# Attention taps and a mixture layer: last rows of x stacked high over low, low parts by TensorE and ScalarE, three partial sums left to VectorE, and a new order of steps

## The chip, the cores and the metric

One NeuronCore of a Trainium2 chip runs the whole kernel. The time is device microseconds per execution; lower is better. PE is TensorE's matmul, PEld its weight load, DVE is VectorE, ACT ScalarE, POOL GpSimd, SP the engine that issues most transfers.

## The reference

```python
def _attn_ref(x, weight_gen):            # x: 8 x 4160 x 192, weight_gen: 8 x 4160 x 8 x 7
    w = softmax(weight_gen over its 7 taps)
    x_unf = the 7 rows x[s-6 .. s], zeros ahead of the start
    out[s, head, :] = sum over k of w[s, head, k] * x_unf[s, k, head, :]

def _moe_ref(x, w_in, w_out, g_ln):      # x: 33280 x 192, w_in: 192 x 1024, w_out: 1024 x 192
    h = x @ w_in
    e = np.exp(h - h_max)
    sm = e / (np.sum(e, axis=-1, keepdims=True) + 1e-09)
    solu = h * sm
    ln = (solu - mean(solu)) / np.sqrt(var(solu) + 1e-06) * g_ln
    return ln @ w_out
```

`w_in`, `w_out` and `g_ln` come as float64 (`x` and `weight_gen` as float32). The first function's output is the second's `x`.

## The kernel before, in words

The 33280 rows are laid out as 128 partitions of 260 consecutive rows (`RUN` = 260). A *tile* t is row t of all partitions: 128 rows. Four tiles make a *group* (`TG`; the first four tiles are two groups of two), sixteen a chunk, which is what a transfer of `x` and of the taps brings.

The work of a group (`attention`, step `attA`, lines 133 to 141) is on GpSimd: multiply seven shifted rows by their weights (`pr`), add rows 3 to 5 onto rows 0 to 2, and add once more, so that two rows per output are left in `half`. VectorE adds these two (`fin`, line 365) into `a`; ScalarE copies the last 64 columns so that `a` has 256 columns (`dup`, line 371): 128, the last 64, and the last 64 again.

For a pair of tiles TensorE transposes `a` into `pa` in PSUM (`xT`, line 382), two blocks of 128 rows each: the first 128 columns of x, and the last 64 twice. To keep the precision of float32, x and `w_in` are split into a high part (rounded to the matmul's format) and a low rest. ScalarE rounds `pa` to `x_hi` (`xhi`, line 390). The rest is made in one of two ways: TensorE subtracts by a matmul with minus the identity (`xn`, line 397), and ScalarE copies the result to `x_lo` (`xlo`, line 404); or VectorE subtracts in one instruction (`xld`, line 411). With `VECTOR_PAIRS = 2` every second pair goes the second way.

The first product (`mm1`, lines 421 and 426) makes a tile's `h`, 128 x 1024 in PSUM, two halves of 512. The first 128 rows of x take six matmuls (high by high, high by low, low by high, for each half). The last 64 rows take six more, of 64 rows each: `wb_hi` and `wb_lo` hold the first 512 columns on the upper 64 partitions and the last 512 on the lower 64, and the two matmuls of a pair use the upper and the lower half of the array.

Then, per tile: VectorE's maximum (`max`, 440) and two small steps (`vb` 444, `vr` 449), ScalarE's exponential into `e` (`exp`, 453), VectorE's product with `e` in place (`solu`, 459), ScalarE's squares (`sq`, 465) and high half in 16 bits (`hi`, 472), VectorE's low half (`lo`, 476), a transposing transfer on SP's queue (`tr`, 484), the second product by 24 matmuls into the one PSUM buffer `po` (`mm2`, 528) and ScalarE's scaling out of it (`out`, 539). Once in four tiles eight small steps make the scales (`f0` to `f7`, VectorE's in line 496). `h` has three buffers, `hl` three, `hlT` six, `a` three, `half` two.

Each engine works through its instructions in the order in which they are written. That order comes from a planner, `issue_order`: it lists every step with its engine, a cost and the steps before it, walks through time, and on each engine takes of the steps that are ready the one with the smallest key, the tile's number plus a number of the table `URGENCY`.

Of the kernel before, what the change touches and what calls it, by code (L numbers as in the profile page):

```python
# [26 lines left out]
def tile_kernel(ctx: ExitStack, tc: tile.TileContext, x, weight_gen, w_in, w_out, g_ln, out):  # L27
# [102 lines left out]
    def attention(xt, wt, t, n, half):  # L130

        pr = att.tile([P, K, TG, D], F32, name="pr", bufs=1)[:, :, :n]
        nc.gpsimd.tensor_tensor(  # L133
            out=window(pr, 0, [(TG * D, K), (HG, n * H), (1, HG)]),
            in0=window(xt, t * D, [(D, K), (HG, n * H), (1, HG)]),
            in1=window(wt, t * HK, [(1, K), (K, n * H), (0, HG)]),
            op=ALU.mult,
        )
        nc.gpsimd.tensor_tensor(out=pr[:, :3], in0=pr[:, :3], in1=pr[:, 3:6], op=ALU.add)  # L139

        nc.gpsimd.tensor_tensor(  # L141
            out=half, in0=window(pr, 0, [(2 * TG * D, 2), (D, n), (1, D)]),
            in1=window(pr, TG * D, [(5 * TG * D, 2), (D, n), (1, D)]), op=ALU.add,
        )
# [31 lines left out]
    minus = const.tile([P, P], F32R, name="minus")  # L176
    nc.vector.tensor_scalar_mul(minus, ident, -1.0)
# [42 lines left out]
    wb_hi = const.tile([P, FH], F32R, name="wb_hi")  # L220
    wb_lo = const.tile([P, FH], F32R, name="wb_lo")

    def last_rows(step):
        if step < 3:
            first["b"] = float_of_double("b", raw_b, FH, step)
        elif step == 3:
            nc.scalar.copy(wb_hi, first["b"])
        elif step == 4:
            nc.vector.tensor_tensor(
                out=wb_lo, in0=first["b"], in1=wb_hi.bitcast(F32), op=ALU.subtract  # L230
            )

# [160 lines left out]
    def subtract_high(t):  # L393

        pa, hi = x_parts[t]
        for n in range(2):
            nc.tensor.matmul(
                pa[:, n], minus, hi[:, n], start=False, stop=n == 1, skip_group_check=True
# [9 lines left out]
    def low_x_on_vector(t):  # L408
        pa, hi = x_parts.pop(t)
        lo = small.tile([P, 2, 2, P], F32R, name="x_lo", bufs=2)  # L410
        nc.vector.tensor_tensor(out=lo, in0=pa, in1=hi.bitcast(F32), op=ALU.subtract)  # L411
        for i in range(2):
            xt_of[t + i] = hi[:, :, i, :], lo[:, :, i, :]

    def first_product(t):
# [3 lines left out]
        for fs in halves:  # L419
            for n, (lhs, rhs) in enumerate(((hi, wa_hi), (hi, wa_lo), (lo, wa_hi))):  # L420
                nc.tensor.matmul(h[:, fs], lhs[:, 0, :], rhs[:, fs], start=n == 0, stop=False)  # L421

        for n, (lhs, rhs) in enumerate(((hi, wb_hi), (hi, wb_lo), (lo, wb_hi))):
            for f, fs in enumerate(halves):
                rows = slice(f * D2, (f + 1) * D2)
                nc.tensor.matmul(  # L426
                    h[:, fs], lhs[rows, 1, :], rhs[rows], start=False, stop=n == 2,
                )
# [121 lines left out]
    def at_chunk(op, *args):  # L550
# [3 lines left out]
        attA=attend, attB=lambda t: None, fin=last_sum, dup=copy_columns, xT=transpose_x,  # L554
        xhi=high_x, xn=subtract_high, xlo=low_x, xld=low_x_on_vector, mm1=first_product,
# [3 lines left out]
    for n in range(5):  # L559
# [22 lines left out]
    for op, t in issue_order(RUN, starts, group, stat_group, LOADS):  # L582
# [4 lines left out]
URGENCY = dict(  # L587
    a00=146.3, a01=114, a02=105.5, a03=52.4, a04=58.5, a10=-4.3, a11=-0.8, a12=-8.4, a13=73.8,
    a14=25.5, attA=-2.8, attB=-19.6, b0=129.4, b1=-57.8, b2=-0.3, b3=52.7, b4=-112.9, c00=44.6,
    c01=2.8, c02=-91.1, c10=-93.1, c11=-37.1, c12=-89.4, c20=-34.5, c21=-4.7, c22=16.6, c30=-144.9,  # L590
    c31=12.4, c32=-106.7, dup=8.7, exp=-126.7, f0=126.6, f1=-167.6, f2=7.7, f3=-16.5, f4=2.1,
    f5=-0.2, f6=-129.7, f7=-140.1, fin=-6.2, hi=27.1, lo=-2, lw=157.1, lx0=-8.4, lx1=-95.6,
    lx2=125.7, lx3=8.5, max=40, mm1=26.6, mm2=33.6, od=-17.4, out=4.8, p30=-113.1, p31=-64.5,
    p4=-117.2, p5=143.6, p6=-0.8, p70=179.3, p71=-15.2, p80=-6.7, p81=15.1, q00=3.8, q01=-15.7,
    q02=16.8, q10=-99.3, q11=-14.1, q12=5, q20=-108.4, q21=-65.1, q22=0.2, q30=110, q31=144.7,
    q32=51.3, solu=-130.8, sq=374, t0=10.4, t1=3.2, t2=84, t3=121.1, t4=-15.6, t5=26.9, t6=2.8,
    tr=-113, vb=-142.7, vr=-62.5, xT=24.7, xhi=-12, xld=-20.5, xlo=3.7, xn=-4.4,
)


def issue_order(run, starts, group, stat_group, loads):

    PE, DVE, ACT, SP, POOL = range(5)
    SAME, CROSS = (25, 127, 143, 0, 102), 130
    free = [3000, 5900, 5000, 12000, 9050]  # L610
    steps, number = [], {}

    def add(name, t, engine, cost, *after, ready=0):
        number[name, t] = len(steps)
        steps.append((name, t, engine, cost, [x for x in after if x[1] >= 0], ready))

    def once(name, engine, cost, *after, ready=0):
        add(name, 0, engine, cost, *((x, 0) for x in after), ready=ready)
# [28 lines left out]


    def chunk_of(t):
        return max(c for c in range(len(starts) - 1) if starts[c] <= t)  # L650

    def last_group(c):

        if c < 0:
            return ("attA", -1)
        return ("attA", max(t for t in range(starts[c], starts[c + 1]) if group(t)))

    for c in range(1, len(starts) - 1):
        t, before = starts[c], starts[c - 1] if c > 1 else -1
        short = starts[c + 1] - t < 16  # L660
        if c > 1:
            add("lw", t, SP, 1270, last_group(c - 3))
            add("lx0", t, SP, 1540, last_group(c - 2))
            for n in range(1, loads):
                add(f"lx{n}", t, SP, 1540, (f"lx{n - 1}", t))
        n = (starts[c + 1] - t) * 8
        on = (DVE, POOL, ACT, DVE, ACT, DVE, POOL)
        wide = 60 + 7.3 * n
        costs = (wide, 13.5 * n, 100 + 6 * n, wide, 100 + n, 60 + 6.3 * n, 13.5 * n)
        for k in range(7):  # L670
            if k:
                add(f"t{k}", t, on[k], costs[k], (f"t{k - 1}", t))
            elif c > 1:
                add("t0", t, on[k], costs[k], ("lw", t), ("t6", before))
            else:
                add("t0", t, on[k], costs[k], ready=12000)
# [24 lines left out]

    for t in range(0, run, 2):
        add("xT", t, PE, 500, ("dup", group_of[t]), low_of(t - 2))
        add("xhi", t, ACT, 478, ("xT", t), ("mm1", t - 3))
        if on_vector(t):
            add("xld", t, DVE, 600, ("xhi", t), ("mm1", t - 3))
        else:
            add("xn", t, PE, 250, ("xhi", t))
# [132 lines left out]
```

## Time and profile before

| what | value |
|---|---|
| median of 3 runs | 1350.38 us (1350.15 to 1352.19) |
| span of the profiled execution | 1350.0 us |
| mean granted TensorE clock | 0.989 |
| PE, DVE, ACT, POOL busy | 1255.5, 1227.7, 1123.4, 1247.3 us |
| tiles, groups | 260, 66 |

A row of the groups by line reads: line, engine, operation, output <- inputs, shapes, xcount | busy us in all, mean ns of one | idle time of the engine just ahead of these instructions, and what ended most of it. A row of a timeline reads: start us, length us, engine, line, operation, count, and in brackets idle time before it. Starts of matmuls are recorded, their ends are modelled and overlap. A row of busy times by stretch reads: stretch, its length, busy us and instructions of PE, PEld, DVE, ACT and POOL, clock, share of the transfers, GB/s.

### The profile page before, as it was taken

Reading aid. Unit: us, or ns where it says so; the run is one execution under the profiler, and the core shown is the slowest. Engines: PE = TensorE matmul, PEld = TensorE weight load, DVE = VectorE, ACT = ScalarE, POOL = GpSimd, SP = SyncE. Lnnn points to the kernel's source line nnn. Section 1 sums busy time; section 2 is a strip of 40 time slices with the busy share of each in tenths; the row PEclk is TensorE's granted clock in tenths of the full one; section 3 lists DMA queues with packets and bytes.
Section 4 is the critical chain, followed back from the end, with each engine's and each line's share of the span. In section 5 each row is a group of like instructions: output and inputs, shape, how many; then the busy total and the mean of one; then the engine's idle time right before and its main releaser. Section 6 shows DMA issues by size and latency. Waiting matters only on the chain.

```text
span 1350.0 us, 26629 instructions
## 1 busy us (share of the span) xinstructions
PE 1255.5 (93%) x10028; PEld 988.3 (73%) x10028; DVE 1227.7 (91%) x2068; ACT 1123.4 (83%) x2231; POOL 1247.3 (92%) x242
## 2 busy tenths in 40 slices
PE   0698899999999999999999999999999999999997
PEld 0466677777777777777777777777777777777776
DVE  5999799999999999999999999999999999999984
ACT  2688698888888888988888888889888888888885
POOL 5999999999999999999999999999999999999800
PEclk9799899999999999999999999999999999999999
DMA  5378559786877779797777978697787979767675
GB/s 179 86 183 182 120 106 220 140 199 125 173 154 159 173 145 195 137 200 137 162 165 140 200 130 206 120 184 160 138 193 131 204 131 171 148 133 133 120 135 114
DMA packets 565313, 210.37 MB, mean 156 GB/s; under 512 B 544456, under 2 KB 545864, under 8 KB 565184
## 3 DMA queue, kind: packets, MB, share of 16 engines
q1 hardware_dynamic: 563208, 206.55, 74.3%
q10 hardware_dynamic: 1976, 2.12, 0.6%
q8 instruction: 79, 1.29, 0.4%
q14 instruction: 50, 0.41, 0.1%
HBM read 46.15 MB, written 25.56 MB: 53 GB/s over the span
## 4 chain that ended last, share of the span: by engine, by line
DVE 31%; ACT 23%; POOL 19%; issue 15%; PE 9%; DMA 2%; ACTq 0%; SPq 0%; DVEq 0%; POOLq 0%
POOL pr L133 10%; DVE h L459 10%; ACT hl L472 7%; DVE hl L476 7%; ACT e L465 7%; DVE stats L440 7%; POOL pr L139 6%; ACT e L453 5%; PE po L528 4%; DVE a L365 3%; PE h L421 3%; POOL half L141 2%; PE h L426 2%; ACT ot L539 1%; DVE x_lo L411 1%
## 5 line engine op out<-in xcount | busy, mean ns | idle before, releaser
L133 POOL TENSOR_TENSOR pr<-xt,wt 128x5376 f32<-128x5376 f32 (+1 forms) x66 | 631.5, 9568 | 2.7
L528 PE MATMUL po<-w_hl,hlT 128*128 128x192 f16 x6192 | 557.9, 247 | 24.2 <-ACT ot L539 22.9
L528 PEld LDWEIGHTS <-hlT 128*128 128x128 f16 x6240 | 515.2, 98 | 81.0 <-issue 77.3
L472 ACT ACTIVATE hl<-h 128x1024 f16<-128x1024 f32 x260 | 268.3, 1033 | 103.5 <-DVE stats L496 62.2
L476 DVE SCALAR_TENSOR_TENSOR hl<-h,hl 128x1024 f16<-128x1024 f32 x260 | 316.4, 1219 | 41.7 <-ACT e L465 37.0
L459 DVE SCALAR_TENSOR_TENSOR h<-h,stats,e 128x1024 f32<-128x1024 f32 x260 | 334.4, 1286 | 18.1 <-ACT e L453 7.6
L139 POOL TENSOR_TENSOR pr<-pr 128x2304 f32<-128x2304 f32 (+1 forms) x66 | 332.9, 5044 | 5.2
L453 ACT ACTIVATE e<-h,stats 128x1024 f32<-128x1024 f32 x260 | 293.2, 1128 | 35.4 <-DVE stats L440 30.5
L440 DVE TENSOR_REDUCE stats<-h 128x1 f32<-128x1024 f32 x260 | 315.9, 1215 | 6.1 <-PE h L426 5.9
L465 ACT ACTIVATE e<-h,stats 128x1024 f32<-128x1024 f32 x260 | 293.1, 1128 | 6.9 <-DVE hl L476 6.6
L421 PE MATMUL h<-wa_hi,x_hi 128*128 128x512 f32 x520 | 225.3, 433 | 22.7 <-ACT e L465 7.9
L141 POOL TENSOR_TENSOR half<-pr 128x1536 f32<-128x1536 f32 (+1 forms) x66 | 226.0, 3424 | 5.2
L421 PE MATMUL h<-wa_hi,x_lo 128*128 128x512 f32 x520 | 207.4, 399 | 1.3 <-ACT x_lo L404 1.3
L421 PE MATMUL h<-wa_lo,x_hi 128*128 128x512 f32 x520 | 206.1, 396 | 0.0
L426 PE MATMUL h<-wb_hi,x_hi 64*128 64x512 f32 x520 | 131.5, 502 | 0.0
L421 PEld LDWEIGHTS h<-wa_hi,x_hi 128*128 128x128 f32 x520 | 98.9, 190 | 43.3 <-ACT e L465 10.5
L539 ACT ACTIVATE ot<-po,stats 128x192 f32<-128x192 f32 x258 | 112.1, 434 | 9.5 <-PE po L528 9.4
L426 PEld LDWEIGHTS h<-wb_hi,x_hi 64*128 64x128 f32 x520 | 48.7, 184 | 96.5 <-issue 96.5
L365 DVE TENSOR_REDUCE a<-half 128x768 f32<-128x1536 f32 (+1 forms) x66 | 116.4, 1764 | 1.5 <-POOL half L141 1.5
L421 PEld LDWEIGHTS h<-wa_hi,x_lo 128*128 128x128 f32 x520 | 98.4, 189 | 25.5 <-ACT x_lo L404 3.0
L382 PE MATMUL pa<-ident,a 128*128 128x128 f32 x520 | 84.7, 284 | 31.5 <-DVE a L365 29.1
L421 PEld LDWEIGHTS h<-wa_lo,x_hi 128*128 128x128 f32 x520 | 99.5, 191 | 11.8
(78 smaller groups left out, 1155.2 us busy)
## 6 DMA issues: line engine op xcount, KB each, us to landing
out_dram<-ot SPq DMA_DIRECT2D x65, 384.0 KB, 3.2
xt<-in_x_dram SPq DMA_DIRECT2D x30, 576.0 KB, 4.7
xt<-in_x_dram SPq DMA_DIRECT2D x30, 480.0 KB, 4.4
wt<-in_weight_gen_dram SPq DMA_DIRECT2D x15, 448.0 KB, 4.7
hlT<-hl SPq DMA_TRANSPOSE x260, 4.5
xt<-in_x_dram SPq DMA_DIRECT2D x3, 384.0 KB, 5.4
raw_a<-in_moe_w_in_dram ACTq DMA_DIRECT2D x2, 512.0 KB, 6.8
raw<-in_moe_w_out_dram ACTq DMA_DIRECT2D x1, 768.0 KB, 11.3
```

Source lines behind the costliest of these rows:

```text
L133: nc.gpsimd.tensor_tensor(out=window(pr, 0, [(TG * D, K), (HG, n * H), (1, HG)]), in0=window(xt, t * D, [(D, K), (HG, n * H), (1, HG)]), i ...
L139: nc.gpsimd.tensor_tensor(out=pr[:, :3], in0=pr[:, :3], in1=pr[:, 3:6], op=ALU.add)
L141: nc.gpsimd.tensor_tensor(out=half, in0=window(pr, 0, [(2 * TG * D, 2), (D, n), (1, D)]), in1=window(pr, TG * D, [(5 * TG * D, 2), (D, n), ...
L421: nc.tensor.matmul(h[:, fs], lhs[:, 0, :], rhs[:, fs], start=n == 0, stop=False)
L426: nc.tensor.matmul(h[:, fs], lhs[rows, 1, :], rhs[rows], start=False, stop=n == 2,)
L440: nc.vector.tensor_reduce(stat(t, NMAX), h_of[t], axis=AX.X, op=ALU.max, negate=True)
L453: nc.scalar.activation(e, h_of[t], AF.Exp, bias=stat(t, NMAX), accum_out=stat(t, Z))
L459: nc.vector.scalar_tensor_tensor(out=h, in0=h, scalar=stat(t, SIGMA), in1=e, op0=ALU.mult, op1=ALU.mult, accum_out=stat(t, M))
L465: nc.scalar.activation(e_of.pop(t), h_of[t], AF.Square, bias=stat(t, M), scale=-float(FF), accum_out=stat(t, Q),)
L472: nc.scalar.activation(hl[:, 0, :], h_of[t], AF.Copy, scale=2.0**14)
L476: nc.vector.scalar_tensor_tensor(out=hl[:, 1, :], in0=h_of[t], scalar=2.0**14, in1=hl[:, 0, :], op0=ALU.mult, op1=ALU.subtract,)
L528: nc.tensor.matmul(po[:, :D], hlT[:, half * NJ + j, :], w2_hl[:, j, w, :], start=n == 0, stop=n == len(terms) - 1,)
```

## The change

*Three rows left over.* In every second full group (`rows_left`) the second addition writes its three rows to `half`, a last one adds row 6 to the first of these, and VectorE sums three rows instead of two.

*Low parts.* The way over VectorE is gone: every pair goes through `xn` and `xlo`.

*Stacked rows.* `minus` has a second block whose upper 64 rows are zero. In the block with the last 64 columns twice, only the lower copy is therefore reduced by its high part, so that `x_lo[:, 1]` holds the high part over the low part: 128 rows. `wb` holds the last rows of `w_in` twice, all 1024 columns, on the upper and the lower partitions; four transfers at the start (`b5`) put them there. The first product is then ten matmuls of 128 rows, the two halves of a term one after the other.

*Order.* Costs, gaps between engines and transfers in the planner are new, it may wait a little for a more urgent step (`PATIENCE`), and the table is new.

```diff
@@ attention
+        if half.shape[1] == 3:
+            nc.gpsimd.tensor_tensor(out=half, in0=pr[:, :3], in1=pr[:, 3:6], op=ALU.add)
+            nc.gpsimd.tensor_tensor(
+                out=half[:, 0], in0=half[:, 0], in1=pr[:, 6], op=ALU.add
+            )
+            return
@@
-    nc.vector.tensor_scalar_mul(minus, ident, -1.0)
+    minus = const.tile([P, 2, P], F32R, name="minus")
+    nc.vector.tensor_scalar_mul(minus[:, 0], ident, -1.0)
+    nc.vector.tensor_scalar_mul(minus[:D2, 1], ident[:D2], 0.0)
+    nc.vector.tensor_scalar_mul(minus[D2:, 1], ident[D2:], -1.0)
@@ last_rows
+        elif step == 5:
+            for f in range(2):
+                for k in range(2):
+                    nc.sync.dma_start(
+                        wb.bitcast(F32)[k * D2 : (k + 1) * D2, :, f * FH : (f + 1) * FH],
+                        wb_part.bitcast(F32)[f * D2 : (f + 1) * D2],
+                    )
@@
+    def rows_left(t):
+        return 3 if t >= TG and t // TG % 2 else 2
@@ attend
-        half = att.tile([P, 2, TG, D], F32, name="half", bufs=2)[:, :, :n]
+        half = att.tile([P, 3, TG, D], F32, name="half", bufs=2)[:, : rows_left(t), :n]
@@ subtract_high
-                pa[:, n], minus, hi[:, n], start=False, stop=n == 1, skip_group_check=True
+                pa[:, n], minus[:, n], hi[:, n], start=False, stop=n == 1, skip_group_check=True
@@
-    def low_x_on_vector(t):
-        pa, hi = x_parts.pop(t)
-        lo = small.tile([P, 2, 2, P], F32R, name="x_lo", bufs=2)
-        nc.vector.tensor_tensor(out=lo, in0=pa, in1=hi.bitcast(F32), op=ALU.subtract)
...
@@ first_product
-        for fs in halves:
-            for n, (lhs, rhs) in enumerate(((hi, wa_hi), (hi, wa_lo), (lo, wa_hi))):
-                nc.tensor.matmul(h[:, fs], lhs[:, 0, :], rhs[:, fs], start=n == 0, stop=False)
-
-        for n, (lhs, rhs) in enumerate(((hi, wb_hi), (hi, wb_lo), (lo, wb_hi))):
-            for f, fs in enumerate(halves):
-                rows = slice(f * D2, (f + 1) * D2)
+        terms = (
+            (hi[:, 0, :], wa_hi), (hi[:, 0, :], wa_lo), (lo[:, 0, :], wa_hi),
+            (lo[:, 1, :], wb_hi), (lo[:, 1, :], wb_lo),
+        )
+        for n, (lhs, rhs) in enumerate(terms):
+            for fs in halves:
                 nc.tensor.matmul(
-                    h[:, fs], lhs[rows, 1, :], rhs[rows], start=False, stop=n == 2,
+                    h[:, fs], lhs, rhs[:, fs], start=n == 0, stop=n == len(terms) - 1
                 )
@@ the planner
-URGENCY = dict(
-    a00=146.3, a01=114, a02=105.5, a03=52.4, a04=58.5, a10=-4.3, a11=-0.8, a12=-8.4, a13=73.8,
...
+URGENCY = {
+    "a00": -123.8, "a01": 46.1, "a02": 390.2, "a03": -57.2, "a04": 272.4, "a10": -120.8,
...
+PATIENCE = (132, 164, 167, 1430, 294)
...
-        add("mm1", t, PE, 2460, low_of(t), ("sq", t - 3), ("lo", t - 3), *after)
+        add("mm1", t, PE, 2320, 70, ("xhi", pair), ("xlo", pair, -900), ("sq", t - 3), ("lo", t - 3), *after)
...
-        add("mm2", t, PE, 2170, ("tr", t), *after)
+        add("mm2", t, PE, 1923, 218, ("tr", t), *after)
```

What moves on TensorE, by one tile's first product and what stands behind it, early in the run (`h` is the tile's buffer, `pa` the pair's transposes). Before:

```order
L421 MATMUL h_1223<-wa_hi_128,x_hi_1176 128x512
L421 MATMUL h_1223<-wa_lo_129,x_hi_1176 128x512
L421 MATMUL h_1223<-wa_hi_128,x_lo_1191 128x512
L421 MATMUL h_1223<-wa_hi_128,x_hi_1176 128x512
L421 MATMUL h_1223<-wa_lo_129,x_hi_1176 128x512
L421 MATMUL h_1223<-wa_hi_128,x_lo_1191 128x512
L426 MATMUL h_1223<-wb_hi_130,x_hi_1176 128x512 x2
L426 MATMUL h_1223<-wb_lo_131,x_hi_1176 128x512 x2
L426 MATMUL h_1223<-wb_hi_130,x_lo_1191 128x512 x2
L382 MATMUL pa_1244<-ident_109,a_1118 128x128 x4
```

And now, with the transposes ahead of a first product and the subtraction behind it:

```order
L401 MATMUL pa_2034<-ident_109,a_1994 128x128 x4
L437 MATMUL h_2041<-wa_hi_130,x_hi_1856 128x512 x2
L437 MATMUL h_2041<-wa_lo_131,x_hi_1856 128x512 x2
L437 MATMUL h_2041<-wa_hi_130,x_lo_1886 128x512 x2
L437 MATMUL h_2041<-wb_132,x_lo_1886 128x512 x4
L416 MATMUL pa_2034<-x_hi_2052,minus_117 128x256 x2
```

`x_lo` is now needed by the last six of ten matmuls, where it was needed by the third, and the transposes `pa_2034` belong to a pair that is multiplied later.

What moves on VectorE in the middle of the run (440 and 451 are the maximum, 476 and 487 the low half, 459 and 470 the product with `e`, 365 and 384 the sum over `half`, 496 and 507 a small step of the scales). Before:

```order
L476 SCALAR_TENSOR_TENSOR hl_7817<-h_7702,hl_7817 128x1024
L459 SCALAR_TENSOR_TENSOR h_7768,stats_134<-h_7768,stats_134,e_7839 128x1024
L496 TENSOR_REDUCE stats_134<-stats_134 128x4
L440 TENSOR_REDUCE stats_134<-h_7822 128x1
L411 TENSOR_TENSOR x_lo_7890<-pa_7847,x_hi_7878 128x512
L444 TENSOR_REDUCE stats_134<-stats_134 128x1
L476 SCALAR_TENSOR_TENSOR hl_7882<-h_7768,hl_7882 128x1024
L449 RECIPROCAL stats_134<-stats_134 128x1
L365 TENSOR_REDUCE a_7911<-half_7641 128x4x192
L459 SCALAR_TENSOR_TENSOR h_7822,stats_134<-h_7822,stats_134,e_7892 128x1024
```

And now:

```order
L451 TENSOR_REDUCE stats_136<-h_7534 128x1
L455 TENSOR_REDUCE stats_136<-stats_136 128x1
L460 RECIPROCAL stats_136<-stats_136 128x1
L487 SCALAR_TENSOR_TENSOR hl_7587<-h_7472,hl_7587 128x1024
L470 SCALAR_TENSOR_TENSOR h_7534,stats_136<-h_7534,stats_136,e_7605 128x1024
L451 TENSOR_REDUCE stats_136<-h_7594 128x1
L455 TENSOR_REDUCE stats_136<-stats_136 128x1
L460 RECIPROCAL stats_136<-stats_136 128x1
L487 SCALAR_TENSOR_TENSOR hl_7644<-h_7534,hl_7644 128x1024
L470 SCALAR_TENSOR_TENSOR h_7594,stats_136<-h_7594,stats_136,e_7649 128x1024
L507 TENSOR_REDUCE stats_136<-stats_136 128x4
L384 TENSOR_REDUCE a_7682<-half_7434 128x4x192
```

The subtraction of line 411 is gone, the two small steps follow the maximum directly, and the sum over `half` stands behind a product and not between two steps of one tile.

More of the change, by code (lines that the diff above doesn't have):

```diff
@@ L601, in issue_order @@
[L601 to L618, printed above, removed]
+URGENCY = {
[14 rows of a table added]
+}
@@ L646, in issue_order @@
         once("p8" + half, DVE, 929, "p7" + half)
[L649 to L660, printed above, removed]
-        if c > 1:
[L662 to L676, printed above, removed]
@@ L679, in issue_order @@
-    groups = [t for t in range(run) if group(t)]
-    group_of = {t: g for g in groups for t in range(g, g + group(g))}
+    for c in range(1, chunks):
+        t, before, n = starts[c], starts[c - 1] if c > 1 else -1, (starts[c + 1] - starts[c]) * 8
+        if c > 1:
+            add("lw", t, SP, 60, 0, last_group(c - 3), dma=1270)
+            for k in range(loads):
+                add(f"lx{k}", t, SP, 60, 0, last_group(c - 2), *([(f"lx{k - 1}", t)] if k else []), dma=1540)
+        steps = (
+            (DVE, 60 + 7.2 * n, 92), (POOL, 120 + 12.4 * n, 55), (ACT, 70 + 6 * n, 110),
+            (DVE, 60 + 7.3 * n, 83), (ACT, 100 + 0.8 * n, 115), (DVE, 60 + 6.2 * n, 87),
+            (POOL, 120 + 12.5 * n, 55),
+        )
+        for k, (engine, busy, more) in enumerate(steps):
+            after = [(f"t{k - 1}", t)] if k else [("lw", t), ("t6", before)] if c > 1 else []
+            add(f"t{k}", t, engine, busy, more, *after, ready=0 if c > 1 else 12000)
@@ L681, in issue_order @@
     for i, t in enumerate(groups):
-        c, full = chunk_of(t), group(t) == 4
-        after = [("attB", groups[i - 1])] if i else []
+        c, part, three = chunk_of(t), group(t) / 4, rows_left(t) == 3
+        after = [("fin", groups[i - 2] if i > 1 else -1)]
         if c:
@@ L749, in issue_order @@
-    for i, step in enumerate(steps):
-        for x in step[4]:
-            then[number[x]].append(i)
-            count[i] += 1
-    key = [t + URGENCY.get(name, 0) for name, t, *_ in steps]
-    later, now = [[] for _ in free], [[] for _ in free]
+            add("f0", t, ACT, 97, 116, *(("exp", u, -160) for u in tiles))
+            add("f1", t, DVE, 70, 87, ("f0", t), *(("vr", u) for u in tiles))
+            add("f2", t, ACT, 97, 116, ("f1", t))
+            add("f3", t, DVE, 70, 87, ("f2", t), *(("sq", u) for u in tiles))
@@ new lines, in plan @@
+            add("f4", t, ACT, 347, 116, ("f3", t))
+            add("f5", t, DVE, 70, 87, ("f4", t))
+            add("f6", t, ACT, 282, 105, ("f5", t), ("p4", 0))
+            add("f7", t, DVE, 70, 87, ("f6", t))
+        if t % 4 == 3:
+            add("od", t, SP, 60, 0, ("out", t), dma=1092)
+    number = {(name, t): i for i, (name, t, *_) in enumerate(raw)}
+    steps = []
+    for name, t, engine, busy, done, after, ready, dma in raw:
+        links = []
+        for source, when, *slack in after:
+            i = number[source, when]
+            gap = 0 if raw[i][2] == SP else hop.get((raw[i][2], engine), 0) + late.get((source, name), 0)
+            links.append((i, gap + sum(slack)))
+        twin = number[{"sq": "lo", "lo": "sq"}[name], t] if name in ("sq", "lo") else -1
+        steps.append((name, t, engine, busy, done, links, ready, dma, twin))
@@ new lines, in plan, with urgency, issue_order @@
+    return steps
+TURN = {
+    ("xT", "mm2"): 136, ("mm2", "xT"): 58, ("mm1", "xT"): 20, ("mm1", "xn"): 20, ("mm1", "mm1"): 20,
+    ("xn", "mm2"): 24,
+}
+def urgency(name, t):
+    u = URGENCY.get(name, 0)
+    return t + (u[t % len(u)] if isinstance(u, tuple) else u)
+def issue_order(steps):
+    then, count, ready = [[] for _ in steps], [len(s[5]) for s in steps], [s[6] for s in steps]
+    for i, step in enumerate(steps):
+        for k, gap in step[5]:
+            then[k].append((i, gap))
+    key = [urgency(name, t) for name, t, *_ in steps]
+    engines = range(len(PATIENCE))
+    later, now = [[] for _ in engines], [[] for _ in engines]
+    free, last = [0] * len(engines), [""] * len(engines)
@@ L763, in issue_order @@
             (free[e] if now[e] else max(free[e], later[e][0][0]), e)
-            for e in range(len(free)) if now[e] or later[e]
+            for e in engines if now[e] or later[e]
         ]
```

197 lines of the change are left out of this document (93 added, 104 removed), and 13 rows, old and new, of the table URGENCY.

## The prediction

> **What bounds the kernel now.** I read, in this order: the busy times of the page, the instructions grouped by line for the steady stretch 200 to 1200 us, the stretches at the end, and TensorE's timeline over three tiles. Durations are those of the one profiled execution, whose span is 1350.0 us; the median of the runs is 0.4 us above it. Less than 0.2% of that (2.7 us) a measurement cannot tell from no change.
>
> ```profile
> span 1350.0 us, 26629 instructions
> PE 1255.5 (93%) x10028; PEld 988.3 (73%) x10028; DVE 1227.7 (91%) x2068; ACT 1123.4 (83%) x2231; POOL 1247.3 (92%) x242
> ```
>
> Four engines lie within ten points of each other, so busy shares alone name no bound. The steady stretch does (grouped by line, 200 to 1200 us):
>
> ```profile
> L133 POOL TENSOR_TENSOR pr<-xt,wt 128x5376 f32<-128x5376 f32 x52 | 505.1, 9713 | 2.2
> L139 POOL TENSOR_TENSOR pr<-pr 128x2304 f32<-128x2304 f32 x52 | 266.3, 5122 | 4.1
> L141 POOL TENSOR_TENSOR half<-pr 128x1536 f32<-128x1536 f32 x52 | 180.7, 3475 | 4.1
> L440 DVE TENSOR_REDUCE stats<-h 128x1 f32<-128x1024 f32 x205 | 249.2, 1216 | 4.1 <-PE h L426 3.9
> L528 PE MATMUL po<-w_hl,hlT 128*128 128x192 f16 x4921 | 440.7, 246 | 10.4 <-ACT ot L539 9.3 <-DMA out_dram<-ot 0.5
> L421 PE MATMUL h<-wa_hi,x_hi 128*128 128x512 f32 x410 | 175.9, 429 | 10.2 <-DVE stats L444 5.8 <-ACT e L465 3.8 <-DVE hl L476 0.4
> L421 PE MATMUL h<-wa_hi,x_lo 128*128 128x512 f32 x410 | 162.2, 396 | 0.2 <-ACT x_lo L404 0.2
> L397 PE MATMUL pa<-x_hi,minus 128*128 128x256 f32 x102 | 25.2, 328 | 3.6 <-ACT x_hi L390 3.5
> L453 ACT ACTIVATE e<-h,stats 128x1024 f32<-128x1024 f32 x205 | 231.7, 1130 | 27.5 <-DVE stats L440 23.7 <-DVE stats L449 2.2 <-DVE stats L496 0.4
> ```
>
> In 1000 us VectorE takes 205 row maxima, one per tile: 4.88 us a tile. GpSimd finishes 52 groups of four: 19.2 us a group, 4.81 us a tile, and its idle column (2.2, 4.1, 4.1) names no releaser. So GpSimd never waits, and yet the tiles come out more slowly than it makes them: the other three engines fall slowly behind. The busy times by stretch show the same at the end (columns: stretch, then PE, PEld, DVE, ACT, POOL busy, clock):
>
> ```profile
> 200.00:1200.00 1000.00, 974.41 (x7892) 769.86 (x7890) 940.91 (x1574) 866.27 (x1715) 989.73 (x180) 1.00 0.79 163
> 1250.00:1300.00 50.00, 48.37 (x402) 38.75 (x400) 45.52 (x77) 43.10 (x84) 27.97 (x6) 1.00 0.70 125
> 1300.00:1350.00 50.00, 42.32 (x374) 35.37 (x372) 28.93 (x54) 32.08 (x67) 0.00 (x0) 0.95 0.59 124
> ```
>
> GpSimd has stopped by about 1278, some 72 us before the end. What sets the time is the loop of TensorE, VectorE and ScalarE. TensorE's timeline over three tiles shows which of them is nearest its limit:
>
> ```profile
> 600.86 0.48 PE L397 MATMUL pa<-x_hi,minus 128*128 128x256 f32 x2
> 601.18 0.40 PE L421 MATMUL h<-wa_hi,x_hi 128*128 128x512 f32 x1
> 601.41 0.39 PE L421 MATMUL h<-wa_lo,x_hi 128*128 128x512 f32 x1
> ...
> 602.34 0.39 PE L421 MATMUL h<-wa_hi,x_lo 128*128 128x512 f32 x1
> 602.66 0.50 PE L426 MATMUL h<-wb_hi,x_hi 64*128 64x512 f32 x2
> 603.00 0.39 PE L426 MATMUL h<-wb_lo,x_hi 64*128 64x512 f32 x2
> 603.23 0.39 PE L426 MATMUL h<-wb_hi,x_lo 64*128 64x512 f32 x2
> 603.54 2.15 PE L528 MATMUL po<-w_hl,hlT 128*128 128x192 f16 x24
> ...
> 607.06 0.50 PE L421 MATMUL h<-wa_hi,x_hi 128*128 128x512 f32 x1 [0.92 <-ACT e L465]
> 607.39 0.39 PE L421 MATMUL h<-wa_lo,x_hi 128*128 128x512 f32 x1
> ...
> 618.36 0.66 PE L382 MATMUL pa<-ident,a 128*128 128x128 f32 x4
> 618.85 2.14 PE L528 MATMUL po<-w_hl,hlT 128*128 128x192 f16 x24
> ...
> 621.21 0.39 PE L421 MATMUL h<-wa_hi,x_hi 128*128 128x512 f32 x1
> ```
>
> Ends of matmuls overlap, so I read starts only. From 607.06 to 621.21 there are three tiles with their transposes and one subtraction and no bracket of idle time: 14.15 us, 4.72 a tile. That is TensorE's work; the pace is 4.88, so it waits 0.16 us a tile (3%). The rows above name the waits they can see: 10.4 us before the second product, which waits until ScalarE has emptied the one buffer `po`; 10.2 before the first product, for VectorE and ScalarE to free `h`; 3.6 for the high part. Each is a wait for an engine that is not full, but is doing something else first. TensorE at 97% with waits made by the order is my reading of the bound.
>
> **The change, part by part.** Rows for what it touches (whole run, by shape):
>
> ```profile
> L141 POOL TENSOR_TENSOR half<-pr 128x768 f32<-128x768 f32 x2 | 3.6, 1808 | 0.2
> L365 DVE TENSOR_REDUCE a<-half 128x768 f32<-128x1536 f32 x64 | 114.5, 1789 | 0.0
> L365 DVE TENSOR_REDUCE a<-half 128x384 f32<-128x768 f32 x2 | 1.9, 960 | 1.5 <-POOL half L141 1.5
> L411 DVE TENSOR_TENSOR x_lo<-pa,x_hi 128x512 fp32r<-128x512 f32 x65 | 44.4, 683 | 2.2 <-ACT x_hi L390 2.1
> L404 ACT CAST x_lo<-pa 128x512 fp32r<-128x512 f32 x65 | 39.4, 606 | 1.5 <-PE pa L397 1.5
> ```
>
> *Three rows left over.* In 32 of the 64 full groups the last GpSimd addition shrinks from 3475 to 1808 ns: 32 x 1.667 = 53 us less on GpSimd, 0.83 a group on average, so 18.4 a group or 4.59 a tile. In these groups the middle addition writes `half`, so it needs that buffer one instruction earlier; the buffer was freed a group before. Since GpSimd is ahead, the gain is worth nothing in the steady part; it brings the first tiles sooner, three such groups among the first six, 5 us. VectorE pays: 768 elements took 960 ns and 1536 took 1789, so 2304 should take 1789 + 829 = 2618, 32 x 0.83 = 27 us more. Below nothing it cannot fall, and twice that would be 53.
>
> *Low parts.* VectorE loses 65 x 683 = 44 us, net 18 less with the longer sums (0.07 a tile). ScalarE gains 65 x 606 = 39 us (0.15 a tile). By the stretch 200 to 1200, VectorE was busy 940.91/205 = 4.59 a tile and now 4.52, ScalarE 866.27/205 = 4.23 and now 4.38: VectorE keeps the higher load of the two. TensorE gains 65 subtractions, 601.18 - 600.86 = 0.32 each: 21 us, on the path.
>
> *Stacked rows.* The first product goes from six full-height slots and three slots of half-height pairs to ten full-height ones. A full slot takes 0.23 (601.18 to 601.41). The half-height part runs from 602.57, where the last full slot ends, to 603.54: 0.97 for three slots, because there is an extra 0.09 before, 0.11 inside and 0.08 after. The weight loads show why (TensorE's loads):
>
> ```profile
> 602.65 0.19 PEld L426 LDWEIGHTS h<-wb_hi,x_hi 64*128 64x128 f32 x2 [0.36 <-issue]
> 603.54 1.93 PEld L528 LDWEIGHTS <-hlT 128*128 128x128 f16 x24 [0.35 <-issue]
> ```
>
> A load is not drawn ahead of the matmul when the height changes, on the way in and on the way out. With one height throughout, four slots take 4 x 0.23 = 0.93 instead of 0.97: 10 us less over 260 tiles. Bounds: 13 us less, if the last slot hides its successor's load fully; and 60 us more, if the 0.28 of gaps belong to something else and stay, since one slot more is 0.23 a tile. I take the low end: the two rows tie the gaps to the height.
>
> The Trainium skill, "TensorEngine Tiling (Array Packing)", section Theoretical Speedup, gives up to twofold for a contraction of 64 or less, which speaks against stacking: by that rule alone the tile grows by a slot, 60 us, and the kernel would be slower. Its section Key Properties says that changing the tiling mode drains TensorE; by that rule the stacking wins the drains back, as the two rows above have it.
>
> *Order on TensorE.* Behind a second product the first slot of a tile is longer, 607.39 - 607.06 = 0.33 against 0.23. In the order before, 167 first products follow a second product directly, now 55, since subtraction and transposes now stand in that place; 112 x 0.1 = 11 us less, where the subtraction's 0.32 holds the same extra already. Work on TensorE: 21 - 10 - 11 = 0, so 4.72 a tile stays.
>
> *Order of steps.* This is the term that decides. VectorE's old order shuffles maximum, low half and the small steps from tile to tile; the new one repeats maximum, two small steps, low half of the tile before, product with e. The transposes of a pair are issued mostly four tiles ahead of the first product (77 of 130), before mostly two (100 of 130). A wait is bounded by 0 below and by today's 0.16 a tile, or more, above. I take 0.02, nearer the lower end: the named waits are waits for an engine busy elsewhere, and at 4.74 a tile VectorE (4.52) keeps 5% free and ScalarE (4.38) 8%. Late next is GpSimd, which will begin to wait for free buffers; that costs nothing until its slack of 4.74 - 4.59 is gone.
>
> *Start.* The stacked weights add four transfers on the SP queue behind the second half of `b`:
>
> ```profile
> 23.31 0.68 DVE L229 TENSOR_TENSOR wb_lo<-h,wb_hi 128x512 fp32r<-128x512 f32 x1
> 41.67 0.48 PE L421 MATMUL h<-wa_hi,x_hi 128*128 128x512 f32 x1
> xt<-xt SPq DMA_DIRECT2D x1, 576.0 KB, 10.2
> ```
>
> `wb_lo` is ready at 24.0; a transfer within SBUF took 10.2 us, so they land by about 36, ahead of the first product at 41.67. Behind them in SP's queue stand only loads for later chunks. If that cover failed, the first product would be up to 10 us later, but the second group of tiles still sets the pace there. I cost it at nothing.
>
> *Sum.* The pace goes from 4.88 to 4.72 + 0.02 = 4.74. Over the 236 tiles after the first 20 and before the last four: 236 x 0.14 = 33 us. With 5 us at the start: 38. 1350.4 - 38 = 1312 us.
>
> **Rivals.** *The slots cost what they look like* (slower). The gaps of 0.28 stay with ten full slots: TensorE's tile is 4.72 + 0.23 for the slot + 0.04 for the part of the subtraction not paid by the 112 shorter first slots = 4.99, with 0.02 of waits 5.01; 236 x 0.13 = 31 us more, less 5: 1376. It decides once a first product takes over 0.14 more than I say. Against it: the two load rows. It is the way in which the speedup rule of the Trainium skill, "TensorEngine Tiling (Array Packing)", section Theoretical Speedup, would have it.
>
> *ScalarE comes late with the low part* (slower). Now every pair needs high part, subtraction and low part in ScalarE's order, and the third pair of matmuls waits for it. One pass of ScalarE ahead of it is 1.1 us (1130 ns for the exponential); if all 65 added ones came late, 65 x 1.1 = 72 us, against the 38 gained: 1384; it decides from about half of them. Against it: today the matmul on `x_lo` waits 0.2 us in 1000 for it, and the transposes go earlier.
>
> *The waits are not the order's* (no change). If the loop maximum, exponential, product with e sets the pace by its latency, the waits move to other lines, and only start and a little of the load stay: pace 4.83 to 4.90, 1333 to 1355. For it: VectorE was 94% busy in the steady stretch and gets only 0.07 a tile less. Against it: idle time before the maximum is 4.1 us in 1000, so VectorE is not kept waiting for tiles.
>
> *GpSimd's pace is reached* (better). With 4.59 a tile, 236 x 0.29 = 68 and 5: 1277 is the floor.
>
> **Chances.** My forecast, 1290 to 1333: 0.68. Waits come back elsewhere, 1333 to 1355: 0.17, of which 0.11 still faster, 0.05 the same, 0.01 slower. Slots 0.05, ScalarE 0.05, both slower. Below 1290: 0.05. So faster 0.84, same 0.05, slower 0.11. The range 1287 to 1343 holds the forecast and over half of the second case, and reaches towards GpSimd's floor.
>
> **What would show it.** Right: 210 or more row maxima in 1000 us; ten matmuls of a first product in 2.3 to 2.45 us from start to start, and no load with 0.36 of "issue" in it; GpSimd with waits for VectorE, busy near 1194; the three-row sum near 2.6 us; low parts x130 on ScalarE. Wrong: matmuls 0.3 apart, idle time of TensorE on `x_lo`, or as much idle time on `po` and `h` as now under new names.

## The result, and the profile after

The changed kernel takes 1309.33 us (median of 4 runs, 1308.03 to 1309.64) against 1351.29 for the kernel before on the same chip: ratio 0.9685, 95% interval 0.9671 to 0.9699. The profiled execution has a span of 1307.4 us, 1.9 below the median; before it was 1350.0. The 42.6 us between the two spans are explained below.

The head of the page, busy time by engine:

```profile
span 1307.4 us, 25808 instructions
PE 1236.5 (95%) x9638; PEld 1070.7 (82%) x9638; DVE 1234.1 (94%) x2005; ACT 1163.7 (89%) x2296; POOL 1196.3 (92%) x242
```

The stretch 200 to 1200 us, busy times and then groups by line:

```profile
200.00:1200.00 1000.00, 996.26 (x7833) 863.43 (x7831) 973.66 (x1573) 928.89 (x1827) 979.41 (x186) 1.00 0.80 167
L451 DVE TENSOR_REDUCE stats<-h 128x1 f32<-128x1024 f32 x212 | 258.3, 1218 | 3.6 <-PE h L437 3.4
L539 PE MATMUL po<-w_hl,hlT 128*128 128x192 f16 x5077 | 455.3, 246 | 1.4 <-ACT ot L550 0.7
L437 PE MATMUL h<-wa_hi,x_hi 128*128 128x512 f32 x424 | 142.4, 417 | 1.5 <-ACT e L476 1.5
L437 PE MATMUL h<-wa_hi,x_lo 128*128 128x512 f32 x424 | 133.4, 396 | 0.0
L416 PE MATMUL pa<-x_hi,minus 128*128 128x256 f32 x212 | 50.3, 318 | 0.4 <-ACT x_hi L409 0.4
L126 POOL TENSOR_TENSOR wt<-wt,wy 128x896 f32<-128x896 f32 x12 | 21.2, 1770 | 9.9 <-DVE wy L124 6.0 <-DVE stats L455 3.8
```

212 row maxima in 1000 us instead of 205: 4.72 us a tile. TensorE's visible idle time before the second and the first product falls from 10.4 and 10.2 us to 1.4 and 1.5. VectorE is busy 973.66 instead of 940.91, and GpSimd now waits 9.9 us, for VectorE.

Where the time went is read from the start of the maximum of tile 20 and of tile 256 (VectorE's timeline, first before, then after):

```profile
163.93 1.23 DVE L440 TENSOR_REDUCE stats<-h 128x1 f32<-128x1024 f32 x1 [0.86 <-PE h L426]
...
1312.86 1.21 DVE L440 TENSOR_REDUCE stats<-h 128x1 f32<-128x1024 f32 x1
```

```profile
159.21 1.22 DVE L451 TENSOR_REDUCE stats<-h 128x1 f32<-128x1024 f32 x1
...
1274.11 1.23 DVE L451 TENSOR_REDUCE stats<-h 128x1 f32<-128x1024 f32 x1 [0.16 <-PE h L437]
```

The start gives 4.7 us. The 236 tiles between take 1114.9 instead of 1148.9, 34.0 us less: 4.724 a tile instead of 4.868. The end, from tile 256 on, takes 33.3 instead of 37.1: 3.8. The sum is 42.5. This pace to three digits, worked out in the same way, is what the experiments are compared by.

The pieces, whole run by shape:

```profile
L384 DVE TENSOR_REDUCE a<-half 128x768 f32<-128x2304 f32 x32 | 89.8, 2807 | 0.0
L384 DVE TENSOR_REDUCE a<-half 128x768 f32<-128x1536 f32 x32 | 57.2, 1787 | 0.0
L141 POOL TENSOR_TENSOR half<-half,pr 128x768 f32<-128x768 f32 x32 | 58.7, 1834 | 2.5
L423 ACT CAST x_lo<-pa 128x512 fp32r<-128x512 f32 x130 | 76.5, 589 | 1.8 <-PE pa L416 1.8
```

### The profile page after: what moved, and what is told of

It reads as the page before. It is cut to its first block, busy times and chain, and to the rows that moved or that the text cites. A ratio compares the mean times of both kernels' runs of the same rounds, so it can differ in the third digit from the quotient of the medians.

```text
span 1307.4 us, 25808 instructions
## 1 busy us (share of the span) xinstructions
PE 1236.5 (95%) x9638; PEld 1070.7 (82%) x9638; DVE 1234.1 (94%) x2005; ACT 1163.7 (89%) x2296; POOL 1196.3 (92%) x242
## 4 chain that ended last, share of the span: by engine, by line
PE 63%; DVE 19%; ACT 8%; issue 6%; DMA 4%; SPq 1%; ACTq 0%; POOL 0%; POOLq 0%
PE h L437 31%; PE po L539 26%; DVE h L470 5%; DVE stats L451 5%; DVE a L384 3%; PE pa L401 3%; ACT e L464 3%; ACT hl L483 2%; DMA wt<-in_weight_gen_dram 2%; PE pa L416 2%; DVE hl L487 1%; ACT e L476 1%; DMA hlT<-hl 1%; ACT ot L550 1%; DVE stats L455 0%
## 5 line engine op out<-in xcount | busy, mean ns | idle before, releaser
L437 PE MATMUL h<-wb,x_lo 128*128 128x512 f32 x1040 | 286.6, 397 | 0.0
L437 PEld LDWEIGHTS h<-wb,x_lo 128*128 128x128 f32 x1040 | 197.3, 190 | 47.1
L437 PE MATMUL h<-wa_hi,x_hi 128*128 128x512 f32 x520 | 175.5, 418 | 6.9 <-ACT e L476 6.9
L145 POOL TENSOR_TENSOR pr<-pr 128x2304 f32<-128x2304 f32 (+1 forms) x34 | 169.4, 4982 | 2.7
L437 PE MATMUL h<-wa_hi,x_lo 128*128 128x512 f32 x520 | 164.7, 398 | 4.3 <-ACT x_lo L423 4.3
L140 POOL TENSOR_TENSOR half<-pr 128x2304 f32<-128x2304 f32 x32 | 164.1, 5128 | 2.5
L437 PE MATMUL h<-wa_lo,x_hi 128*128 128x512 f32 x520 | 162.7, 394 | 0.0
L384 DVE TENSOR_REDUCE a<-half 128x768 f32<-128x2304 f32 (+1 forms) x66 | 148.9, 2257 | 0.0
L147 POOL TENSOR_TENSOR half<-pr 128x1536 f32<-128x1536 f32 (+1 forms) x34 | 115.2, 3389 | 2.7
L437 PEld LDWEIGHTS h<-wa_hi,x_hi 128*128 128x128 f32 x520 | 79.0, 190 | 10.2 <-ACT e L476 9.4
```

The source lines that it names most:

```text
L140: nc.gpsimd.tensor_tensor(out=half, in0=pr[:, :3], in1=pr[:, 3:6], op=ALU.add)
L384: nc.vector.tensor_reduce(columns(t)[:, :, :D], half.rearrange("p j t d -> p t d j"), axis=AX.X, op=ALU.add)
L437: nc.tensor.matmul(h[:, fs], lhs, rhs[:, fs], start=n == 0, stop=n == len(terms) - 1)
```

## The experiments

All medians stand beside the kernel before on the same chip (1351.3 to 1351.9 us). The changed kernel's order is kept in e3, e4, e7, e8 and e9; the order before is kept in e5, e6 and e10.

**e1: old instructions, new order.** The functions are those of the kernel before; only the planner is the new one.

```diff
-        xlo=low_x, mm1=first_product,
+        xn=lambda t: None if t // 2 % 2 else subtract_high(t),
+        xlo=lambda t: low_x_on_vector(t) if t // 2 % 2 else low_x(t),
```

> The instructions of the kernel before (two rows left by GpSimd, VectorE subtracts in every second pair, pairs of half-height matmuls) issued in the order of the changed kernel. Theory (the gain is the order's, which removes TensorE's waits, and GpSimd's shorter sum only keeps it from becoming the bound): TensorE's waits go, but GpSimd still needs 4.81 us a tile and now binds it: 1325 to 1340 us, 211 or fewer row maxima in 1000 us, and little idle time before the first and second products. Rival A (the order alone is the whole gain): 1305 to 1315. Rival B (the lighter work on GpSimd and VectorE is the gain, the order nothing): 1345 to 1355.

1340.9 us, ratio 0.9923 (0.9908 to 0.9938), 4.846 a tile: a quarter of the gain, one microsecond above the theory's range. GpSimd was busy 989.73 of 1000 us, as in the kernel before, and now VectorE waits for it in this stretch, which it did not there:

```profile
DVE a L368 <- POOL half L141: 20.6, 21, 2.3
```

The pace stays 0.04 above GpSimd's 4.81 because this order sums a group ever earlier ahead of its tiles: the sum starts 15.4 us ahead of the maximum at tile 20 and 24.5 at tile 256.

**e2: new instructions, old planner.** The functions are the changed ones, the planner is that of before, and the four transfers are issued right behind `b4`.

```diff
-VECTOR_PAIRS = 2
+VECTOR_PAIRS = 0
```

> The instructions of the changed kernel (three rows in every second group, all low parts by TensorE and ScalarE, ten full-height matmuls) in an order made by the planner of before, with its costs and its table, and the four transfers of the stacked weights behind the second half of b. Theory (the order is the gain): TensorE's work is the same, GpSimd's gain is not used, ScalarE has 39 us more in an order that was not made for it: 1335 to 1360. Rival B (lighter work is the gain): 1300 to 1320.

1395.99 us, ratio 1.0328 (1.0304 to 1.0352), 5.073 a tile: far above both expectations. The new instructions in this order are no gain; the waits between VectorE and ScalarE are still there, and two of the three are larger (waits, 200 to 1200 us; the first three rows were 49.6, 22.7 and 30.0 in the kernel before):

```profile
ACT hl L482 <- DVE stats L506: 45.2, 57, 1.5
DVE hl L486 <- ACT e L475: 40.9, 53, 1.2
ACT hl L482 <- DVE h L469: 38.9, 54, 1.7
PEld pa L415 <- ACT x_hi L408: 32.0, 48, 2.0
```

The old planner made another order here than in the kernel before, so this run tells that the changed instructions need an order made for them, not how good exactly the old one was.

**e3: the changed kernel with two rows left in every group.**

```diff
-        half = att.tile([P, 3, TG, D], F32, name="half", bufs=2)[:, : rows_left(t), :n]
+        half = att.tile([P, 3, TG, D], F32, name="half", bufs=2)[:, :2, :n]
```

> The changed kernel, its order kept, with two rows left in every group as before: GpSimd has 53 us more, VectorE some 30 us less. Theory: GpSimd at 4.81 us a tile becomes the bound where TensorE held 4.72: 236 x 0.09 = 21 us and 5 at the start, 1325 to 1340; GpSimd without waits. If GpSimd's gain is worth nothing in the steady part, as the prediction said: 1307 to 1316. If VectorE were the bound: 1275 to 1295.

1338.78 us, ratio 0.9904 (0.9888 to 0.9921), 4.849 a tile, in the theory's range: without GpSimd's shorter sum, 29 of the 42 us are lost, though VectorE has less to do. GpSimd does not wait any more.

```profile
DVE a L384 <- POOL half L147: 45.3, 42, 3.1
```

**e4: the changed kernel with half-height pairs.** `first_product`, `minus` and `wb` are those of before.

```diff
-            (lo[:, 1, :], wb_hi), (lo[:, 1, :], wb_lo),
...
+        for n, (lhs, rhs) in enumerate(((hi, wb_hi), (hi, wb_lo), (lo, wb_hi))):
+            for f, fs in enumerate(halves):
+                rows = slice(f * D2, (f + 1) * D2)
```

> The changed kernel, its order kept, with the last 64 rows in pairs of half-height matmuls as before (x low parts still all by TensorE and ScalarE, four transfers at the start left out). Theory (the gaps at a change of height eat the saved slot): 0.04 us a tile more on the engine that binds, 1312 to 1322. Rival (a pair of half-height matmuls in one slot is a slot saved): 0.23 us a tile less on TensorE, as far as the next bound allows, 1275 to 1300.

1318.79 us, ratio 0.9758 (0.9744 to 0.9773), 4.755 a tile: stacking is worth 9.5 us, as the theory has it. The Trainium skill, "TensorEngine Tiling (Array Packing)", section Theoretical Speedup, gives the pairs up to twofold. Inside a pair the trace of the kernel before agrees, two matmuls in one slot of 0.23 us; with the gaps around them the pairs are the slower form.

**e5: the kernel before with a shorter last addition on GpSimd.**

```diff
+        ) if not short else nc.gpsimd.tensor_tensor(
+            out=half[:, 0], in0=pr[:, 0], in1=pr[:, 6], op=ALU.add
```

> The kernel before, in every second full group GpSimd's last addition makes one row instead of two, and VectorE sums that row with itself, so rows 1 to 5 of the seven are left out of these groups' output: GpSimd has 53 us less to do, all else as before. Theory (before, GpSimd is no bound): only the first tiles come sooner, 1342 to 1351. Rival (GpSimd binds before, being 99% busy): 1295 to 1315.

1341.49 us, ratio 0.9928 (0.9911 to 0.9944), half a microsecond below the theory's range. The maximum of tile 20 starts at 156.0 instead of 163.9, and the pace is 4.862, where it was 4.868: nearly all that 53 us less on GpSimd bring in the old order is the start.

**e6: the kernel before with ten matmuls.**

```diff
-            for n, (lhs, rhs) in enumerate(((hi, wa_hi), (hi, wa_lo), (lo, wa_hi))):
+            for n, (lhs, rhs) in enumerate(((hi, wa_hi), (lo, wa_hi))):
```

> The kernel before without the product of the high part of x with the low part of the first 128 rows of w_in: ten matmuls a tile in the first product instead of twelve, 0.46 us a tile less on TensorE. Theory (TensorE's work and the waits of its order set the pace): the pace falls until GpSimd's 4.81 a tile holds it, 1325 to 1338. Rival (the loop of VectorE and ScalarE sets the pace by its latency): 1343 to 1351.

1349.92 us, ratio 0.9994 (0.9985 to 1.0003), 4.867 a tile: the rival's range. The theory fell here: 260 x 0.46 = 120 us less on TensorE change nothing. GpSimd's 4.81 would have left room for 236 x 0.06 = 14 us, and VectorE never waits for GpSimd in this stretch, so it is not GpSimd that hides a gain. The time came back as idle time (groups by line, 200 to 1200 us):

```profile
L528 PE MATMUL po<-w_hl,hlT 128*128 128x192 f16 x4920 | 439.7, 246 | 58.3 <-ACT ot L539 56.1 <-DMA out_dram<-ot 1.1
L421 PE MATMUL h<-wa_hi,x_hi 128*128 128x512 f32 x409 | 176.0, 430 | 22.4 <-DVE stats L444 12.3 <-ACT e L465 7.3 <-DVE hl L476 1.9
L397 PE MATMUL pa<-x_hi,minus 128*128 128x256 f32 x102 | 25.3, 330 | 20.8 <-ACT x_hi L390 20.7
L472 ACT ACTIVATE hl<-h 128x1024 f16<-128x1024 f32 x205 | 212.0, 1034 | 81.2 <-DVE stats L496 49.7 <-DVE h L459 31.1
L476 DVE SCALAR_TENSOR_TENSOR hl<-h,hl 128x1024 f16<-128x1024 f32 x205 | 249.5, 1220 | 27.4 <-ACT e L465 24.8 <-ACT hl L472 1.3
```

ScalarE and VectorE wait for each other as much as in the kernel before (its rows, same stretch):

```profile
L472 ACT ACTIVATE hl<-h 128x1024 f16<-128x1024 f32 x205 | 211.9, 1034 | 80.2 <-DVE stats L496 49.6 <-DVE h L459 30.0
L476 DVE SCALAR_TENSOR_TENSOR hl<-h,hl 128x1024 f16<-128x1024 f32 x206 | 250.6, 1219 | 23.7 <-ACT e L465 22.7
```

**e10: e5 with a shorter sum on VectorE.** This follows from e6: if not TensorE, then VectorE with its waits.

```diff
-            columns(t)[:, :, :D], half.rearrange("p j t d -> p t d j"), axis=AX.X, op=ALU.add
+            columns(t)[:, :, :D], half[:, :1].rearrange("p j t d -> p t d j"), axis=AX.X, op=ALU.add
```

> The kernel before with GpSimd's last addition shortened in every second group, and VectorE summing one row instead of two in all groups (the rest of the seven rows is left out of the output): VectorE has 64 x 0.83 = 53 us less, 0.2 a tile; GpSimd cannot hold the pace above 4.6. Theory, new after the relief of TensorE changed nothing (VectorE's work and its waits for ScalarE set the pace before): from 4.86 to 4.66 to 4.72 a tile, 1293 to 1310 us. Rival (the hand-overs between ScalarE and VectorE in their order set it, whatever VectorE's load): 4.82 to 4.87, 1332 to 1342.

1317.2 us, ratio 0.9745 (0.9731 to 0.976): 24 us below e5, between the two expectations, at 4.756 a tile. VectorE's load did hold the pace. Half of the 53 us is used: TensorE is now nearly full, and VectorE's wait for it ahead of the maximum rises from 3.9 to 10.0 us:

```profile
200.00:1200.00 1000.00, 992.14 (x8081) 787.13 (x8080) 920.59 (x1611) 883.72 (x1754) 976.84 (x186) 1.00 0.82 166
L441 DVE TENSOR_REDUCE stats<-h 128x1 f32<-128x1024 f32 x210 | 255.4, 1216 | 10.6 <-PE h L427 10.0
```

**e12: e1 with e5's addition.** Order and GpSimd's relief together, and nothing else of the change.

```diff
-        attention(xs[c], ws[c], t - starts[c], n, half)
+        attention(xs[c], ws[c], t - starts[c], n, half, t >= TG and t // TG % 2)
```

> The instructions of the kernel before in the changed kernel's order, and GpSimd's last addition shortened in every second group while VectorE sums that one row with itself (rows 1 to 5 left out there): the new order and GpSimd's relief together, without the rest of the change. Alone the order gave 10 us and the relief 10. Theory (the order takes away VectorE's and TensorE's waits, and GpSimd's 4.81 us a tile is all that hid it): 4.72 to 4.76 a tile, 1303 to 1318 us. Rival (the two add up): 1328 to 1335, 4.83 a tile.

1314.22 us, ratio 0.9727 (0.971 to 0.9745), 4.733 a tile: the theory's range. The order alone gave 10 us, the relief alone 10, both together 37. VectorE sums two rows here in all groups, so against the changed kernel its load is higher by 65 subtractions and lower by the longer sums.

**e7, e8 and e9: what binds the changed kernel.** e7 leaves out two matmuls a tile, e8 sums two of the three rows, e9 does both.

```diff
-            (lo[:, 1, :], wb_hi), (lo[:, 1, :], wb_lo),
+            (lo[:, 1, :], wb_hi),
```

```diff
-            columns(t)[:, :, :D], half.rearrange("p j t d -> p t d j"), axis=AX.X, op=ALU.add
+            columns(t)[:, :, :D], half[:, :2].rearrange("p j t d -> p t d j"), axis=AX.X, op=ALU.add
```

> The changed kernel, its order kept, without the product of the stacked rows with the low part of w_in: eight matmuls a tile instead of ten, 0.46 us a tile less on TensorE. Theory (TensorE binds at 4.72 a tile, GpSimd is next at 4.6 and VectorE near it): 4.60 to 4.68 a tile, 1280 to 1298, idle time on TensorE for VectorE or ScalarE. Rival (VectorE or GpSimd already binds): 1303 to 1309.

> The changed kernel, its order kept, with VectorE summing only two of the three rows in the groups of three, so the third row is left out of the output there: VectorE has 32 x 1.0 = 33 us less. Theory (TensorE binds): 1303 to 1309. Rival (VectorE, 97% busy in the steady stretch, binds): 1280 to 1295.

> The changed kernel, its order kept, with both reliefs together: eight matmuls a tile in the first product (the product of the stacked rows with the low part of w_in left out) and two of three rows summed by VectorE. Alone they brought the pace from 4.72 to 4.71 and 4.70 us a tile. Theory (TensorE and VectorE bind together, each holds the pace when the other is relieved; GpSimd's 4.62 is next): 4.63 to 4.67 a tile, 1283 to 1295 us. Rival (the fixed order with its hand-overs holds the pace, or GpSimd already does): 4.69 to 4.71, 1298 to 1304.

| | us | ratio (interval) | a tile |
|---|---|---|---|
| e7, TensorE 0.46 a tile less | 1301.41 | 0.9634 (0.9617 to 0.9651) | 4.710 |
| e8, VectorE 33 us less | 1305.24 | 0.9656 (0.9642 to 0.9671) | 4.705 |
| e9, both | 1287.65 | 0.953 (0.9515 to 0.9545) | 4.654 |

Alone they bring 8 and 4 us; the interval of e8 touches that of the changed kernel. e7 falls between the ranges of its two theories. Its profiled execution took 1305.23 us and the three others 1299.7 to 1301.5, so 4.710 is somewhat above its usual pace. Together (e9, in the theory's range) they bring 22, more than the two added. So each of the two holds the pace when the other is relieved, and in e9 GpSimd is next: it is busy 989 of 1000 us, and VectorE waits for it again, 7.9 us:

```profile
200.00:1200.00 1000.00, 934.33 (x7525) 800.78 (x7523) 961.61 (x1597) 935.09 (x1853) 989.11 (x188) 1.00 0.82 169
```

**e11: the changed kernel, planned anew** with two costs as its trace has them, and a new table.

```diff
-        add("fin", t, DVE, part * (2480 if three else 1697), 92, ...
+        add("fin", t, DVE, part * (2718 if three else 1697), 92, ...
-        add("mm1", t, PE, 2320, 70, ...
+        add("mm1", t, PE, 2328, 70, ...
 TURN = {
+    ("mm2", "mm1"): 85, ("xT", "mm1"): 85,
```

> The changed kernel with another order: in the planner the three-row sum costs 2718 instead of 2480 and a first product behind a second product or a transpose 85 ns more, as the changed kernel's trace has them, and the table of urgencies is chosen anew for these costs. All instructions are the same. Theory (what the changed kernel still waits comes from an order made with two wrong costs): 1290 to 1303 us. Rival (the engines' work holds the pace, 4.72 a tile): 1304 to 1312.

1305.93 us (1305.39 to 1307.07), ratio 0.9663 (0.9647 to 0.968), 4.709 a tile: the rival's range. It is the fastest full kernel here, 3.4 us below the changed one, but the two intervals against the kernel before overlap, so this gain is about what can be told and no more. Putting these two costs right changed little; whether another order would give more is open.

## Why the prediction came out, step by step

*The sum.* 1312 was forecast, 1309.3 measured. The steady part was put at 33 us and gave 34.0. The start was put at 5 and gave 4.7, but that match is luck: the prediction took it from GpSimd's shorter sum, and e3, where GpSimd has its full work again, reaches tile 20 as early as the changed kernel (VectorE's timeline of e3):

```profile
158.43 1.22 DVE L451 TENSOR_REDUCE stats<-h 128x1 f32<-128x1024 f32 x1
```

e1, with the new order alone, reaches it at 164.7, and e4, without the stacked rows, at 159.3. That points to the new way of the low parts, which no run takes by itself. The end was put at nothing and gave 3.8. It belongs to the order: from tile 256 on, e1 takes 33.4 us with the old instructions, and e5, e6 and e10 take 35.9 to 37.2 in the old order.

*The order of steps* was named as the term that decides. It does so only together with GpSimd's relief: alone it gives 10 us (e1), with the relief 37 of the 42 (e12).

*TensorE as the bound* of the kernel before is the step that failed. TensorE's work of 4.72 a tile was read well (e10, with VectorE lightened, runs at 4.76 and TensorE is then busy 992 of 1000 us). But it was not what the kernel before waited for: e6 took a tenth of that work away and won nothing. The waits on TensorE's rows, which the prediction added up, were made by other engines. VectorE's load held the pace, as e10 shows against e5. That VectorE's and ScalarE's waits for each other made up the rest is read from the rows and was not tested alone: 80 us of idle time before the high half in 1000, which stood in the same view, outside the rows that the prediction shows, and was passed over. The rival of a loop that sets the pace was nearer to the kernel before, but the new order did shorten that loop. In it the rows read:

```profile
L483 ACT ACTIVATE hl<-h 128x1024 f16<-128x1024 f32 x212 | 218.2, 1029 | 16.1 <-DVE h L470 14.2 <-DVE stats L507 1.0
L487 DVE SCALAR_TENSOR_TENSOR hl<-h,hl 128x1024 f16<-128x1024 f32 x212 | 258.8, 1221 | 7.8 <-ACT hl L483 5.8 <-ACT e L476 0.3 <-issue 0.3
```

80.2 became 16.1 and 23.7 became 7.8. The forecast time was still near, because with these waits gone TensorE's 4.72 is the next limit, together with VectorE's load (e7 to e9), and that was the number in the sum. That a misread bound still led to this number is partly luck.

*GpSimd's gain worth nothing in the steady part* failed too. It holds in the old order (e5). At 4.72 a tile GpSimd's old 4.81 would have been the bound, as e1 and e3 show; in e3 that costs 29 us. The prediction had both numbers, 4.81 and 4.74, and did not set them side by side.

*The three-row sum* was put at 2618 ns and takes 2807: 32 x 1.02 = 33 us more on VectorE instead of 27. The line through 768 and 1536 elements read was 7% short at 2304. VectorE's load was put too low with it, at 4.52 us a tile; the steady stretch shows 973.66 / 212 = 4.59, so VectorE has 3% free and not 5%. The longer sum explains 0.02 of the difference, and the rest is open.

*Stacked rows* were put at 10 us and measured at 9.5 (e4). The price is the forecast one, as the starts of TensorE's matmuls show:

```profile
601.19 1.09 PE L437 MATMUL h<-wb,x_lo 128*128 128x512 f32 x4
602.12 2.15 PE L539 MATMUL po<-w_hl,hlT 128*128 128x192 f16 x24
...
604.38 0.62 PE L437 MATMUL h<-wa_hi,x_hi 128*128 128x512 f32 x2
604.84 0.62 PE L437 MATMUL h<-wa_lo,x_hi 128*128 128x512 f32 x2
...
609.18 0.71 PE L437 MATMUL h<-wa_hi,x_hi 128*128 128x512 f32 x2
609.73 0.62 PE L437 MATMUL h<-wa_lo,x_hi 128*128 128x512 f32 x2
```

The four slots take 602.12 - 601.19 = 0.93 us where the half-height part took 0.97. Over the steady stretch the second product starts 0.24 us (median) behind the last matmul of a first product, where it was 0.32: the gaps on the way in and out are gone. The weight load of the second product still stands 0.28 us behind the load before it, where 0.35 was (TensorE's loads):

```profile
602.12 1.93 PEld L539 LDWEIGHTS <-hlT 128*128 128x128 f16 x24 [0.28 <-issue]
```

So most of that bracket has nothing to do with the height, and it holds up the matmuls by no more than 0.01 us. The prediction read too much into the load rows; its reading of the starts was right. The Trainium skill's rule of a drain at a change of tiling mode ("TensorEngine Tiling (Array Packing)", section Key Properties) fits the gaps of 0.09 and 0.08 that went. The 0.11 inside the half-height part, where the height does not change, it does not explain.

*Order on TensorE* was put at 11 us less and is nearer 6. A first product behind transposes has the long first slot too: two slots take 609.73 - 609.18 = 0.55 there and 604.84 - 604.38 = 0.46 behind a subtraction. In the traces 86 first products now stand behind transposes, where 40 did, and 57 behind a second product, where 169 did. So 66 became shorter, and not 112, by some 0.09 each. The missing 5 us, 0.02 a tile, are less than a reading of 4.72 from three tiles can tell.

*The rivals.* The slots did not cost a slot (e4). ScalarE was not late with the low part: the matmul on `x_lo` waits 0.0 us in the steady stretch. GpSimd's floor was not reached, but e9 comes close to it.

*The transfers of the stacked weights* were costed at nothing, and rightly. They land in 4.3 us. The maximum of the first tile starts at 47.89 instead of 46.95 us, but e4, which leaves these transfers out, starts it no earlier:

```profile
48.12 1.22 DVE L442 TENSOR_REDUCE stats<-h 128x1 f32<-128x1024 f32 x1 [1.45 <-PE h L428]
```

## What to carry to other kernels

Idle time on the busiest engine says who is late, not that this engine is the bound: look for two engines that wait for each other in turn, and test a bound by taking work away from it, since a relief that comes back as idle time elsewhere was none. When several engines lie within a few per cent, reliefs do not add up, and testing them one at a time misleads: the order and GpSimd's relief gave 10 us each and 37 together. Before writing that one engine's gain is worth nothing, compare its old pace with the new pace that is forecast. And a term that comes out near its forecast is not shown by that: here the start gained what was forecast, without the cause that was named.

## What was not expected of the hardware

The pair of half-height matmuls does run in one slot of 0.23 us, and still a first product with three such pairs is 0.04 us slower than one of ten full-height matmuls (9.5 us over 260 tiles). A VectorE sum over strided rows that reads 768, 1536 and 2304 elements takes 960, 1789 and 2807 ns: the first two sum two rows, the last sums three. From 768 to 1536 elements it costs 829 ns more, from 1536 to 2304, with the third row, 1018.
